# Two of the last batch's transposes moved from TensorE to the DMA engines

## The chip, the cores and the metric

The kernel runs on one core of one Trainium2 chip. The metric is the device time of one execution in microseconds, the median of several runs. A profile of one execution goes with it. In it PE is TensorE's matmul row and PEld its row of weight loads, DVE is VectorE, ACT is ScalarE, POOL is GpSimd, and SP is SyncE, which here only issues DMAs.

## The reference

Two layers stand one behind the other. The first is a causal linear attention with decay over 4 batches, 8 heads, 768 tokens and 64 channels a head, in blocks. The second takes its output x, with the heads laid side by side (4 x 768 x 512), and mixes tokens with weights that are made from x:

```python
# lightning attention, per block of 64 tokens
intra = ((qb @ kb.T) * Dmask) @ vb
inter = (qb * lam_pow) @ kv_state
out[:, :, sl] = intra + inter
kv_state = lam_block * kv_state + (kb * rev_pow).T @ vb

# token mixer
wq, wk = x @ w_q, x @ w_k                   # 512 -> 64
W_tok = scale * einsum('bsd,btd->bst', wq, wk)
mixed = einsum('bst,btd->bsd', W_tok, x)
out = maximum(mixed, 0) @ w_out             # 512 -> 512
```

## The kernel before

**Tiles.** The 32 heads are worked as 16 pairs, numbered n = 4 b + kk: batch b has the pairs 4b to 4b+3. A pair has 128 channels (two heads of 64) and 768 tokens, in six chunks of 128. For a pair the kernel loads q, k and v (DMAs issued by GpSimd that also convert to bf16), turns q and k with TensorE so that channels lie on partitions, makes scores, masks them, makes states, and sums the inner and the outer part in PSUM. `attended` (word `ex`) copies the result into xnat[b], with tokens on partitions. The mixer's projections need x with channels on partitions as well, so `flip` (word `F`, line 427) transposes the six chunks of a pair on TensorE into PSUM, and `flipped` (word `ef`, line 235 through the helper `copy`) copies them into xT[b].

**The mixer of a batch.** `mix_q` (word `Q`, line 449) multiplies xT, four matmuls for the four pairs of a batch in the order kk = 0 to 3, for each half of the tokens; `mix_k` (`K`, line 475) turns a part back to tokens on partitions; `mix_y` (`Y`, line 500) multiplies that with xnat; `mix_m` (`m`, line 524) makes the mixed values, and `mixed_m` (`em`, lines 535 and 537) applies the relu into rmT[b]; `mix_o` (`O`, line 553) multiplies with w_out, and `mixed_o` (`eo`) copies a tile of 128 tokens and stores it by a DMA on SyncE's queue (line 564).

**Two orders of tokens.** q is loaded in a way that puts neighbouring tokens, even and odd, side by side in a row of SBUF. So within a chunk the tokens of one kind stand in the kernel in another order ("the order of the q loads") than in the output. `flip` multiplies with the matrix `order`, not with the identity `ident`, and so puts the tokens of xT back into the order of the output while it transposes. `mix_k` then reads every second column to fit xT to xnat again.

**What sets the order.** It is written by hand: the string ORDER is a list of words, `name.arguments@PSUM-bank:engine`, and each word emits its instructions in that place. Each engine runs its own instructions strictly in order; semaphores hold an instruction until its inputs are there. There are no planned costs or due times. The change concerns the last five lines of ORDER: the pairs 12 to 15 are those of the last batch, b = 3, whose attention ends beside the last mixing steps of batch 2. Its `Q.3.1` and `Q.3.0` are the first words that read xT[3].

The words around the change, with the lines of the profile:

- `ex.12`, `ex.13` and `ex.14` run on ScalarE (`:a`), `ex.15` on VectorE (`:v`); all are line 235, tile xnat.
- `F.12` to `F.15` are line 427; `ef.12` and `ef.14` run on ScalarE, `ef.13` and `ef.15` on VectorE.
- `m.2.0` to `m.2.3` and `em.2.0` to `em.2.3` are the last products and relus of batch 2, `O.1.2` an output tile of batch 1 kept for this place.
- `Q.3.1`, `Q.3.0`, `K.3`, `Y.3` and the words `m.3` and `O.3` are batch 3's mixer, with the output tiles of batch 2 in the gaps.

Of the kernel before, what the change touches and what calls it, by code (L numbers as in the profile page):

```python
# [9 lines left out]
BF16 = mybir.dt.bfloat16  # L10
F32 = mybir.dt.float32
ALU = mybir.AluOpType
ACT = mybir.ActivationFunctionType

B, H, S, D = 4, 8, 768, 64
CH = 128
NCH = S // CH
HD = H * D
DHY = 64
NP = H // 2  # L20
HALF = 3 * CH
# [9 lines left out]
v.13 sv.10:p q.14 k.14 v.14 sv.11:p q.15 k.15 v.15 sv.12:p sv.13:p sv.14:p hold.14 Aq.0@0 dq.2  # L31
eq.0@0 dq.1 Z.5@7 Ak.0@0 dq.3 ek.0@0:v Z.3@7 S0.0@0 sv.0:v S1.0@2 Mc.1.0@2 M0.0@0 Z.3@7 Pw.0@4
Aq.1@5 G.0@4:a Mm.1.0:v Z.1@7 I.0@0 eq.1@5 V.0@0 Ak.1@5 ex.0@0:a ek.1@5:v Z.2@7 F.0@4 sv.1:v
S0.1@0 M0.1@0 Z.1@7 Aq.2@5 Pw.1@2 eq.2@5 G.1@2:a Z.1@7 Ak.2@3 ef.0@4:v S1.1@0 ek.2@3:v M1.1@0
Z.1@7 S0.2@2 S1.2@4 I.1@6 Mc.0.2@2 V.1@6 sv.2:v Mc.1.2@4 Z.1@3 Aq.3@2 ex.1@6:a Mm.1.2:v Pw.2@3
eq.3@2 Ak.3@4 G.2@3:a Mm.0.2:v F.1@5 ek.3@4:a I.2@2 ef.1@5:v V.2@2 sv.3:v S0.3@4 cw.0:a S1.3@6
Qp.0.0@0 Mc.1.3@6 M0.3@4 Pw.3@1 Aq.4@6 G.3@1:a Mm.1.3:v I.3@4 ex.2@2:v V.3@4 Qp.1.0@1 ex.3@4:a
Ak.4@7 eq.4@6 F.2@2 ek.4@7:a F.3@6 ef.2@2:v Qp.0.1@0 eg.3.0@6:a Qp.1.1@1 Qp.0.2@0 eg.3.1@6:v
Qp.0.3@0 Qp.1.2@1 eQ.0.0@0:a Qp.1.3@1 S0.4@6 eQ.0.1@1:a S1.4@2 M0.4@6 Mc.1.4@2 Kh.0.1@1 Kh.0.0@0
Aq.5@4 Ak.5@5 ek2.0.1@1:v ek2.0.0@0:a Mm.1.4:v Y.0@0 ek.5@5:a eq.5@4 YA.0@0:a YB.0@0:v S1.5@4  # L40
M1.5@4 YC.0@0:a m.0.1@1@2 Pw.4@3 eh.0.1.1@2:a m.0.0@0@6 eh.0.1.0@1:v G.4@3:a Aq.6@2 eh.0.0.1@6:a
I.4@4 eq.6@2 eh.0.0.0@0:a S0.5@6 m.0.3@1@3 M0.5@6 V.4@4 eh.0.3.1@3:a Ak.6@2 ex.4@4:a sv.6:v
m.0.2@3@0 eh.0.2.0@3:a F.4@4 ek.6@2:a eh.0.2.1@0:v P.6@3 P.5@5 Gp.6@3 eh.0.3.0@1:a S0.6@6 O.0.4@2
Gp.5@5 Mc.0.6@6 ef.4@4:v S1.6@6 eo.0.4@2:a I.6@0 Mm.0.6:v I.5@4 V.5@4 M1.6@6 Aq.7@2 ex.5@4:a
Ak.7@3 eq.7@2 O.0.5@6 ek.7@3:v V.6@0 eo.0.5@6:v S1.7@2 S0.7@4 M1.7@2 F.5@6 O.0.0@7 ex.6@0:v
O.0.3@2 eo.0.0@7:a M0.7@4 O.0.1@7 ef.5@6:v F.6@3 sv.8:v eo.0.1@7:a P.7@6 Ak.8@4 ef.6@3:a Gp.7@6
Aq.8@7 P.8@5 ek.8@4:a eq.8@7 I.7@0 V.7@0 Gp.8@5 Aq.9@4 ex.7@0:a eo.0.3@2:v Ak.9@5 S0.8@6 ek.9@5:v
# [9 lines left out]
Q.2.0@0 Mc.1.12@6 Q.2.1@1 Mm.0.13:v eQ.2.0@0:a P.13@4 Mm.1.12:v Ak.15@5 eQ.2.1@1:a Gp.13@4 Aq.15@0  # L57
ek.15@5:a Ak.14@1 eq.15@0 Aq.14@4 ek.14@1:a sv.15:v K.2@6 Pw.14@0 eK.2@6:a S0.15@2 eq.14@4 P.12@1
Mc.0.15@2 Y.2@5 Gp.12@1 G.14@0:a P.15@4 YB.2@5:v YA.2@5:a I.13@2 S1.15@0 Gp.15@4 S0.14@6 YC.2@5:a
V.13@2 Mc.0.14@6 M1.15@0 O.1.0@4 ex.13@2:a Mm.0.14:v I.15@0 S1.14@6 Mm.0.15:v eo.1.0@4:a I.12@2  # L60
V.12@2 M1.14@6 V.15@0 ex.12@2:a I.14@4 ex.15@0:v m.2.3@6 V.14@4 F.12@2 em.2.3@6:v ex.14@4:a F.15@3
F.13@0 ef.12@2:a ef.15@3:v F.14@1 m.2.1@6 ef.13@0:v ef.14@1:a m.2.0@4 m.2.2@2 em.2.0@4:v O.1.2@0
em.2.2@2:a Q.3.1@1 em.2.1@6:a Q.3.0@2 eo.1.2@0:a eQ.3.1@1:v O.2.3@3 eQ.3.0@2:a K.3@2 eo.2.3@3:a
O.2.5@0 eK.3@2:v Y.3@1 eo.2.5@0:a O.2.1@0 YA.3@1:v YB.3@1:a YC.3@1:v m.3.0@2 eo.2.1@0:v m.3.1@6
m.3.2@4 em.3.0@2:a O.2.2@1 em.3.2@4:v em.3.1@6:a m.3.3@2 eo.2.2@1:v O.2.0@0 em.3.3@2:a O.2.4@1
eo.2.0@0:v O.3.0@2 eo.2.4@1:a O.3.1@3 eo.3.0@2:a O.3.4@2 eo.3.1@3:a O.3.3@3 eo.3.4@2:v O.3.5@1
eo.3.3@3:a O.3.2@0 eo.3.5@1:a eo.3.2@0:a
"""
# [3 lines left out]
def kernel(  # L72
# [11 lines left out]
    nc = tc.nc  # L84
    mm = nc.tensor.matmul

    consts = ctx.enter_context(tc.tile_pool(name="consts", bufs=1))
    stage = ctx.enter_context(tc.tile_pool(name="stage", bufs=N))
    tsb = ctx.enter_context(tc.tile_pool(name="tsb", bufs=4))
    small = ctx.enter_context(tc.tile_pool(name="small", bufs=2))  # L90
    big = ctx.enter_context(tc.tile_pool(name="big", bufs=2))
# [4 lines left out]
    PS = ps.tile([128, 8, HD], F32, name="ps")  # L96
    PSH = PS.bitcast(BF16)
# [42 lines left out]
    def load_wo(_):  # L140
# [28 lines left out]
        out=ET[:, 0:CH], data0=step, data1=step, initial=0.0, op0=ALU.add, op1=ALU.bypass  # L169
    )  # L170
    for at, n in ((CH, CH), (2 * CH, 2 * CH), (4 * CH, 2 * CH)):
        nc.vector.tensor_tensor(
            out=ET[:, at : at + n], in0=ET[:, 0:n],
# [3 lines left out]
    ident = consts.tile([128, 128], BF16, name="ident")  # L177
    nc.vector.tensor_tensor(
        out=ident.rearrange("e (p r) -> e p r", r=2), in0=natural,
# [4 lines left out]
        out=mask1, in0=ET[:, 0:CH], in1=row.to_broadcast([128, CH]), op=ALU.is_ge  # L184
# [4 lines left out]
    for r in range(2):  # L189
        nc.vector.tensor_tensor(  # L190
            out=token[R[r], :], in0=token[R[r], :],
# [5 lines left out]
        out=order.rearrange("e (p r) -> e p r", r=2), in0=natural,  # L197
# [5 lines left out]
        out=E6, in0=ET[:, ::CH], in1=row.to_broadcast([128, NCH]), op=ALU.add  # L203
# [3 lines left out]
    lamv = lam_all.rearrange("p (k l) -> p k l", l=2)  # L207
    for hl in range(2):
        nc.scalar.activation(out=lncol[R[hl], :], in_=lamv[R[hl], :, hl], func=ACT.Ln)
    pw48 = consts.tile([128, H, NCH], F32, name="pw48")  # L210
    mask2 = mask1.unsqueeze(1).unsqueeze(1).to_broadcast([128, 2, 3, CH])
    Dq = [consts.tile([128, S], BF16, name=f"dq{kk}") for kk in range(NP)]
# [18 lines left out]
    qT, kT, pr, gs = {}, {}, {}, {}  # L231
    xnat, xT = {}, {}

    def copy(eng, to, of):
        return (nc.scalar.copy if eng == "a" else nc.vector.tensor_copy)(out=to, in_=of)  # L235
# [94 lines left out]
    def masked(a):  # L330
        def one(n, o):
            pr[n, a] = tsb.tile([128, 2, HALF], BF16, tag=f"pr{a}", name="pr")
            nc.vector.tensor_tensor(  # L333
                out=pr[n, a].rearrange("j l (c i) -> j l c i", c=3),
                in0=PS[:, o : o + 2, 0:HALF].rearrange("j l (c i) -> j l c i", c=3),
                in1=mask2,
                op=ALU.mult,
            )

        return one  # L340
# [10 lines left out]
        )  # L351


    def states(whole):
        def one(n, o):
            to = PS[:, o, 0 : (NCH - 1) * D].rearrange("e (c f) -> e c f", c=NCH - 1)
            for c in range(NCH - 1):
                end = 2 if c < 2 and not whole else NCH - 1
                for hl in range(2):
                    mm(  # L360
                        to[R[hl], c:end, :],
                        fk[n][:, hl, c, :],
                        vn[n][:, hl, c, :].unsqueeze(1).to_broadcast([128, end - c, D]),
                        start=(c == 0),
                        stop=(c == NCH - 2),
                        skip_group_check=True,
                    )

        return one

    def summed(n, o, eng):
        gs[n] = tsb.tile([128, NCH - 1, D], BF16, tag="gs", name="gs")
        of = PS[:, o, 0 : (NCH - 1) * D].rearrange("e (c f) -> e c f", c=NCH - 1)
        copy(eng, gs[n], of)

    def added(n, o):
        gs[n] = tsb.tile([128, NCH - 1, D], BF16, tag="gs", name="gs")
# [46 lines left out]
    def flip(n, o):  # L424
        b, kk = divmod(n, NP)
        for c in range(NCH):
# [3 lines left out]
                order,  # L430
            )

    def flipped(n, o, eng):
        b, kk = divmod(n, NP)
        copy(eng, xT[b][:, kk, :], PSH[:, o, 0:S])
# [8 lines left out]
    qk, wkn, YA, YB, rmT = {}, {}, {}, {}, {}  # L444
# [24 lines left out]
            qk[b] = small.tile([128, S], BF16, tag="qk", name="qk")  # L469
        copy(eng, qk[b][:, n * HALF : (n + 1) * HALF], PS[:, o, 0:HALF])  # L470

    def mix_k(b, o, chunks=range(NCH)):
        for c in chunks:
            for r in range(2):
                mm(
                    PS[R[r], o, c * DHY : (c + 1) * DHY],
                    qk[b][:, c * CH + r : (c + 1) * CH : 2],
                    ident[:, R[1 - c // 3]],
                    start=(c == chunks[0]),
                    stop=(c == chunks[-1]),  # L480
                    skip_group_check=True,
                )

    def mix_k_half(b, half, o):
        mix_k(b, o, range(3 * half, 3 * half + 3))
# [27 lines left out]
    def crossed_y(f):  # L513
        def one(b, o, eng):
            if b not in YB:
                YB[b] = small.tile([128, 256], BF16, tag="YB", name="YB")
            copy(eng, YB[b][R[1 - f], :], PS[R[f], o, 0:256])

        return one
# [13 lines left out]
    def relu(eng, to, of):  # L533
        if eng == "a":
            nc.scalar.activation(out=to, in_=of, func=ACT.Relu, scale=1.0 / 8.0)  # L535
        else:
            nc.vector.tensor_scalar(
                out=to, in0=of, scalar1=1.0 / 8.0, scalar2=0.0, op0=ALU.mult, op1=ALU.max
            )

    def mixed_m(b, dd, o, eng):
        if b not in rmT:
            rmT[b] = big.tile([128, 4, 2, HALF], BF16, tag="rmT", name="rmT")
        relu(eng, rmT[b][:, dd], PS[:, o : o + 2, 0:HALF])

    def mixed_m_half(b, dd, n, o, eng):
        if b not in rmT:
            rmT[b] = big.tile([128, 4, 2, HALF], BF16, tag="rmT", name="rmT")
        relu(eng, rmT[b][:, dd, n], PS[:, o, 0:HALF])
# [40 lines left out]
    def zeros(count, o):  # L590
# [9 lines left out]
        q=load_q, k=load_k, v=load_v, wq=load_wq, wk=load_wk, cw=copy_wq, wo=load_wo, hold=hold, dq=make_dq, dv=make_dv,  # L600
        sv=scale_v, Aq=turn_q, Ak=turn_k, eq=turned_q, ek=turned_k, A4q=turn_q4, A4k=turn_k4,
        e4q=turned_q4, e4k=turned_k4, S0=scores(0), S1=scores(1),
        M0=masked(0), M1=masked(1), Mc=drawn, Mm=masked_late, P=states(False), Pw=states(True), G=summed, Gp=added, I=inter, V=values, ex=attended, F=flip,
        ef=flipped, eg=flipped_half, Q=mix_q, eQ=mixed_q, K=mix_k, eK=mixed_k, Kh=mix_k_half, ek2=mixed_k_half, Y=mix_y, YA=mixed_y, YB=crossed_y(0), YC=crossed_y(1), Qp=mix_q_part, m=mix_m,
        em=mixed_m, eh=mixed_m_half, O=mix_o, eo=mixed_o, Oh=mix_o_half, oh=mixed_o_half, Z=zeros,
    )
    for word in ORDER.split():
        piece, _, eng = word.partition(":")
# [34 lines left out]
```

## Time and profile before

| | |
|---|---|
| time, median of 3 runs | 101.39 us (101.31 to 101.42) |
| span of the profiled execution | 99.9 us |
| first load issued by GpSimd / last flip ends, by the chain of waits | 1.24 us / 80.03 us |
| flips on TensorE in all | 96 matmuls, 7.3 us busy |
| copies of flips | VectorE 10 of 552 ns, ScalarE 5 of 805 ns, and two halves |
| stores of the output on SyncE's queue | 24, 256 KB each, 2.0 us from issue to landing |

A busy share is an average over the whole span. What the change can be worth is read from the chain of waits, which goes back from the last instruction to what released each, and from the timeline of the stretch from 75 to 85 us, in which the attention of the last four pairs ends and the mixer of the last batch begins.

The line of DMA shares of the page gives the state of the DMA engines in 40 equal slices, in tenths:

```profile
DMA  0999999999999999999999999999910202526782
```

The loads keep all 16 engines at nine tenths until slice 29, that is until about 72 us. After it there are stores alone.

### The profile page before, as it was taken

To read this page: it belongs to the slowest core of one execution; us is meant where nothing else is said; L and a number is where in the kernel's file an instruction comes from. 1 tells how busy PE (TensorE), PEld (TensorE's weight loads), DVE (VectorE), ACT (ScalarE), POOL (GpSimd) and SP (SyncE) were. 2 spreads that over 40 slices of the span, in tenths; PEclk is the share of its full clock that TensorE was granted. 3 is DMA by queue.
4 is the path that set the end of the run, shared out by engine and by line. 5 is a ranking of instruction groups with operands and counts; after the bars stand their busy time and mean duration, and the time that the engine had idled before them with its cause. 6 is when DMAs were issued, how large, how long until landed. Compare 5 with 4: busy or idle time off the path is not lost.

```text
span 99.9 us, 3414 instructions
## 1 busy us (share of the span) xinstructions
PE 90.6 (91%) x1458; PEld 59.4 (59%) x1466; DVE 74.3 (74%) x145; ACT 65.2 (65%) x107; POOL 62.2 (62%) x65
## 2 busy tenths in 40 slices
PE   5999999799998779999999999999999999999930
PEld 3465777678555445757858675866976854434400
DVE  6739596988686996799999899787999964482200
ACT  5585414676877924326798898888978895484440
POOL 5999995889989998999999999940000000000000
PEclk9999999999999966999999999999999999999999
DMA  0999999999999999999999999999910202526782
GB/s 1 98 141 161 164 159 166 161 163 166 164 162 200 173 167 159 165 171 156 164 167 163 163 170 161 162 317 403 361 35 7 105 7 105 210 105 243 282 315 105
DMA packets 67438, 16.60 MB, mean 166 GB/s; under 512 B 63840, under 2 KB 64352, under 8 KB 67424
## 3 DMA queue, kind: packets, MB, share of 16 engines
q0 software_dynamic: 63792, 10.10, 136.8%
q1 hardware_dynamic: 3632, 6.30, 16.8%
q8 instruction: 11, 0.18, 0.7%
q14 instruction: 3, 0.02, 0.1%
HBM read 20.19 MB, written 6.29 MB: 265 GB/s over the span
## 4 chain that ended last, share of the span: by engine, by line
PE 42%; DVE 20%; POOL 20%; DMA 8%; issue 4%; ACT 1%; POOLq 0%; DVEq 0%; ACTq 0%
PE ps L553 18%; DMA fv<-in_v_dram 8%; POOL fk L118 6%; POOL fv L122 6%; POOL fq L114 5%; DVE pr L333 4%; PE ps L360 3%; PE ps L319 3%; DVE fv L240 3%; PE ps L404 3%; PE ps L449 3%; PE ps L524 3%; PE ps L427 2%; DVE pr L349 2%; DVE qT L308 2%
## 5 line engine op out<-in xcount | busy, mean ns | idle before, releaser
L553 PE MATMUL ps<-wo,rmT 128*128 128x512 bf16 x88 | 23.2, 388 | 0.7 <-issue 0.4
L122 POOL DMA_DIRECT2D fv<-in_v_dram x16 | 16.6, 1039 | 2.3 <-DMA fv<-in_v_dram 1.4
L333 DVE TENSOR_TENSOR pr<-ps,mask 128x768 bf16<-128x768 f32 x17 | 16.1, 951 | 1.8 <-PE ps L319 1.8
L235 ACT COPY osb<-ps 128x512 f32<-128x512 f32 x18 | 10.6, 588 | 10.3 <-PE ps L553 10.2
L118 POOL DMA_DIRECT2D fk<-in_k_dram x16 | 16.8, 1049 | 0.3 <-DMA fv<-in_v_dram 0.3
L345 ACT CAST pr<-ps 128x768 bf16<-128x768 f32 x15 | 11.7, 803 | 4.8 <-PE ps L319 4.7
L114 POOL DMA_DIRECT2D fq<-in_q_dram x16 | 14.1, 884 | 0.8 <-POOLq L627 0.8
L553 PEld LDWEIGHTS <-rmT 128*128 128x128 bf16 x96 | 8.6, 99 | 9.7 <-issue 1.3
L240 POOL TENSOR_TENSOR fv<-fv,DvI 128x768 bf16<-128x768 bf16 x9 | 14.0, 1572 | 0.0
L235 ACT CAST xnat<-ps 128x768 bf16<-128x768 f32 x12 | 9.6, 800 | 4.3 <-PE ps L404 4.2
L593 PE MATMUL ps<-blank 128*128 128x128 f32 (+3 forms) x26 | 10.5, 514 | 1.1 <-DVE blank L159 1.1
L308 DVE TENSOR_TENSOR qT<-ps,dq 128x768 bf16<-128x768 bf16 x16 | 8.8, 551 | 1.7 <-PE ps L252 1.5
L349 DVE TENSOR_TENSOR pr<-pr,mask 128x768 bf16<-128x768 bf16 x15 | 9.9, 668 | 0.2
L535 ACT ACTIVATE rmT<-ps 128x768 bf16<-128x768 f32 (+1 forms) x14 | 9.0, 677 | 1.1 <-PE ps L524 0.9
L319 PE MATMUL ps<-qT,kT 64*128 64x128 bf16 x192 | 9.4, 223 | 0.4
L360 PE MATMUL ps<-fv,fk 128*64 128x128 bf16 (+4 forms) x160 | 8.1, 236 | 1.8 <-DVE fv L240 1.3
L252 PE MATMUL ps<-ident,fq 128*64 128x128 bf16 x192 | 8.2, 221 | 0.6 <-DMA fq<-in_q_dram 0.5
L360 PEld LDWEIGHTS <-fk 128*64 128x64 bf16 x160 | 6.4, 114 | 3.9 <-DVE fv L240 1.4
L240 DVE TENSOR_TENSOR fv<-fv,DvI 128x768 bf16<-128x768 bf16 x7 | 7.9, 1134 | 0.7 <-DMA fv<-in_v_dram 0.6
L319 PEld LDWEIGHTS <-kT 64*128 64x128 bf16 x192 | 5.8, 96 | 4.1 <-issue 1.9
L261 PE MATMUL ps<-ident,fk 128*64 128x128 bf16 x192 | 8.2, 221 | 0.0
L404 PE MATMUL ps<-fv,pr 128*128 128x64 bf16 x192 | 8.1, 194 | 0.0
(68 smaller groups left out, 143.8 us busy)
## 6 DMA issues: line engine op xcount, KB each, us to landing
out_dram<-osb SPq DMA_DIRECT2D x24, 256.0 KB, 2.0
fq<-in_q_dram POOLq DMA_DIRECT2D x16, 192.0 KB, 8.0
fk<-in_k_dram POOLq DMA_DIRECT2D x16, 192.0 KB, 8.4
fv<-in_v_dram POOLq DMA_DIRECT2D x16, 192.0 KB, 8.5
wo<-in_moe_w_out_dram POOLq DMA_DIRECT2D x1, 512.0 KB, 9.9
wqk<-in_moe_w_q_dram POOLq DMA_DIRECT2D x1, 64.0 KB, 7.9
wqk<-in_moe_w_k_dram POOLq DMA_DIRECT2D x1, 64.0 KB, 7.6
lam_all<-in_lam_dram SPq DMA_DIRECT2D x1, 4.0 KB, 2.5
```

The costliest lines, as they stand in the source:

```text
L114: nc.gpsimd.dma_start(out=fq[n], in_=rows_q(n))
L118: nc.gpsimd.dma_start(out=fk[n], in_=rows(n, k))
L122: nc.gpsimd.dma_start(out=fv[n], in_=rows(n, v))
L235: return (nc.scalar.copy if eng == "a" else nc.vector.tensor_copy)(out=to, in_=of)
L240: (nc.gpsimd if eng == "p" else nc.vector).tensor_tensor(out=vn[n], in0=fv[n], in1=DvI[:, 2 * kk : 2 * kk + 2, :].unsqueeze(3).to_broadcas ...
L319: mm(PS[:, o + hl, cc * CH : (cc + 1) * CH], kT[n][R[hl], c], qT[n][R[hl], c], start=True, stop=True, skip_group_check=True,)
L333: nc.vector.tensor_tensor(out=pr[n, a].rearrange("j l (c i) -> j l c i", c=3), in0=PS[:, o : o + 2, 0:HALF].rearrange("j l (c i) -> j l c ...
L345: nc.scalar.copy(out=pr[n, a], in_=PS[:, o : o + 2, 0:HALF])
L349: (nc.gpsimd if eng == "p" else nc.vector).tensor_tensor(out=of, in0=of, in1=mask2, op=ALU.mult)
L360: mm(to[R[hl], c:end, :], fk[n][:, hl, c, :], vn[n][:, hl, c, :].unsqueeze(1).to_broadcast([128, end - c, D]), start=(c == 0), stop=(c == ...
L404: mm(PS[:, o + hl, c * D : (c + 1) * D], pr[n, c // 3][:, hl, (c % 3) * CH : (c % 3 + 1) * CH], vn[n][:, hl, c, :], start=False, stop=(c = ...
L553: mm(PS[:, o, :], rmT[b][:, kt].rearrange("f n i -> f (n i)")[:, t * CH : (t + 1) * CH], wo[:, kt, :], start=(kt == 0), stop=(kt == 3),)
```

## The change

Pairs 12 and 13 are no longer transposed by TensorE. `flip_dma` (word `DF`) issues six DMA transposes a pair on SyncE's queue, each from a 128 x 128 piece of xnat[3] in SBUF straight into xT[3] in SBUF, behind the copies `ex.13` and `ex.12`. The words `F.12`, `F.13`, `ef.12` and `ef.13` are gone. The purpose is to use the DMA engines, which have little to do once the loads have ended, for work that now takes TensorE, a PSUM bank, and a copy on VectorE or ScalarE.

[...] So the whole last batch stays in the order of the q loads: pairs 14 and 15 are flipped with `ident` (`flip_plain`, word `Fi`), `mix_k` reads two contiguous runs of columns in place of every second one (`mix_k_plain`, word `Kc`), and the relu puts the tokens back in order as it writes rmT (`mixed_m_plain`, word `en`), with a step of two elements.

```diff
-V.13@2 Mc.0.14@6 M1.15@0 O.1.0@4 ex.13@2:a Mm.0.14:v I.15@0 S1.14@6 Mm.0.15:v eo.1.0@4:a I.12@2
-V.12@2 M1.14@6 V.15@0 ex.12@2:a I.14@4 ex.15@0:v m.2.3@6 V.14@4 F.12@2 em.2.3@6:v ex.14@4:a F.15@3
-F.13@0 ef.12@2:a ef.15@3:v F.14@1 m.2.1@6 ef.13@0:v ef.14@1:a m.2.0@4 m.2.2@2 em.2.0@4:v O.1.2@0
+V.13@2 Mc.0.14@6 M1.15@0 O.1.0@4 ex.13@2:a DF.13 Mm.0.14:v I.15@0 S1.14@6 Mm.0.15:v eo.1.0@4:a I.12@2
+V.12@2 M1.14@6 V.15@0 ex.12@2:a DF.12 I.14@4 ex.15@0:v m.2.3@6 V.14@4 em.2.3@6:v ex.14@4:a Fi.15@3
+ef.15@3:v Fi.14@1 m.2.1@6 ef.14@1:a m.2.0@4 m.2.2@2 em.2.0@4:v O.1.2@0
...
+    def flip_dma(n):
+        b, kk = divmod(n, NP)
+        for c in range(NCH):
+            nc.sync.dma_start_transpose(
+                out=xT[b][:, kk, c * CH : (c + 1) * CH],
+                in_=xnat[b][:, c, kk * CH : (kk + 1) * CH],
+            )
...
+                if plain:
+                    at = slice(c * CH + r * D, c * CH + (r + 1) * D)
...
+        relu(
+            eng,
+            rmT[b][:, dd].rearrange("f n (c p r) -> f n c r p", c=3, r=2),
+            PS[:, o : o + 2, 0:HALF].rearrange("f n (c r p) -> f n c r p", c=3, r=2),
+        )
```

In the rest of the last batch `K.3` becomes `Kc.3` and the four `em.3` become `en.3`. Two memsets of a small tile `keep` are added at the start; together with two further helpers (`scanned` and the form "single" of `states`) they belong to words that ORDER does not use.

More of the change, by code (lines that the diff above doesn't have):

```diff
@@ L59 @@
 Mc.0.15@2 Y.2@5 Gp.12@1 G.14@0:a P.15@4 YB.2@5:v YA.2@5:a I.13@2 S1.15@0 Gp.15@4 S0.14@6 YC.2@5:a
-V.13@2 Mc.0.14@6 M1.15@0 O.1.0@4 ex.13@2:a Mm.0.14:v I.15@0 S1.14@6 Mm.0.15:v eo.1.0@4:a I.12@2
-V.12@2 M1.14@6 V.15@0 ex.12@2:a I.14@4 ex.15@0:v m.2.3@6 V.14@4 F.12@2 em.2.3@6:v ex.14@4:a F.15@3
-F.13@0 ef.12@2:a ef.15@3:v F.14@1 m.2.1@6 ef.13@0:v ef.14@1:a m.2.0@4 m.2.2@2 em.2.0@4:v O.1.2@0
-em.2.2@2:a Q.3.1@1 em.2.1@6:a Q.3.0@2 eo.1.2@0:a eQ.3.1@1:v O.2.3@3 eQ.3.0@2:a K.3@2 eo.2.3@3:a
+V.13@2 Mc.0.14@6 M1.15@0 O.1.0@4 ex.13@2:a DF.13 Mm.0.14:v I.15@0 S1.14@6 Mm.0.15:v eo.1.0@4:a I.12@2
+V.12@2 M1.14@6 V.15@0 ex.12@2:a DF.12 I.14@4 ex.15@0:v m.2.3@6 V.14@4 em.2.3@6:v ex.14@4:a Fi.15@3
+ef.15@3:v Fi.14@1 m.2.1@6 ef.14@1:a m.2.0@4 m.2.2@2 em.2.0@4:v O.1.2@0
+em.2.2@2:a Q.3.1@1 em.2.1@6:a Q.3.0@2 eo.1.2@0:a eQ.3.1@1:v O.2.3@3 eQ.3.0@2:a Kc.3@2 eo.2.3@3:a
 O.2.5@0 eK.3@2:v Y.3@1 eo.2.5@0:a O.2.1@0 YA.3@1:v YB.3@1:a YC.3@1:v m.3.0@2 eo.2.1@0:v m.3.1@6
-m.3.2@4 em.3.0@2:a O.2.2@1 em.3.2@4:v em.3.1@6:a m.3.3@2 eo.2.2@1:v O.2.0@0 em.3.3@2:a O.2.4@1
+m.3.2@4 en.3.0@2:a O.2.2@1 en.3.2@4:v en.3.1@6:a m.3.3@2 eo.2.2@1:v O.2.0@0 en.3.3@2:a O.2.4@1
 eo.2.0@0:v O.3.0@2 eo.2.4@1:a O.3.1@3 eo.3.0@2:a O.3.4@2 eo.3.1@3:a O.3.3@3 eo.3.4@2:v O.3.5@1
@@ L209 @@
         nc.scalar.activation(out=lncol[R[hl], :], in_=lamv[R[hl], :, hl], func=ACT.Ln)
+    keep = consts.tile([128, NCH - 1], F32, name="keep")
+    nc.vector.memset(keep, 1.0)
+    nc.vector.memset(keep[:, 0:1], 0.0)
     pw48 = consts.tile([128, H, NCH], F32, name="pw48")
@@ L351, in masked_late, with states @@
         )
-    def states(whole):
+    def states(form):
         def one(n, o):
@@ L357, in one @@
             for c in range(NCH - 1):
-                end = 2 if c < 2 and not whole else NCH - 1
+                end = NCH - 1
+                if form == "halves" and c < 2:
+                    end = 2
+                if form == "single":
+                    end = c + 1
                 for hl in range(2):
@@ L374, in summed, with scanned @@
         copy(eng, gs[n], of)
+    def scanned(n, o):
+        gs[n] = tsb.tile([128, NCH - 1, D], BF16, tag="gs", name="gs")
+        nc.vector.tensor_tensor_scan(
+            out=gs[n].rearrange("e c f -> e f c"),
+            data0=keep.unsqueeze(1).to_broadcast([128, D, NCH - 1]),
+            data1=PS[:, o, 0 : (NCH - 1) * D].rearrange("e (c f) -> e f c", c=NCH - 1),
+            initial=0.0,
+            op0=ALU.mult,
+            op1=ALU.add,
+        )
     def added(n, o):
@@ L431, in flip, with flip_plain @@
             )
+    def flip_plain(n, o):
+        b, kk = divmod(n, NP)
+        for c in range(NCH):
+            nc.tensor.transpose(
+                PSH[:, o, c * CH : (c + 1) * CH],
+                xnat[b][:, c, kk * CH : (kk + 1) * CH],
+                ident,
+            )
+    def flip_dma(n):
+        b, kk = divmod(n, NP)
+        for c in range(NCH):
+            nc.sync.dma_start_transpose(
+                out=xT[b][:, kk, c * CH : (c + 1) * CH],
+                in_=xnat[b][:, c, kk * CH : (kk + 1) * CH],
+            )
     def flipped(n, o, eng):
@@ L470, in mixed_q, with mix_k @@
         copy(eng, qk[b][:, n * HALF : (n + 1) * HALF], PS[:, o, 0:HALF])
-    def mix_k(b, o, chunks=range(NCH)):
+    def mix_k(b, o, chunks=range(NCH), plain=False):
         for c in chunks:
             for r in range(2):
+                at = slice(c * CH + r, (c + 1) * CH, 2)
+                if plain:
+                    at = slice(c * CH + r * D, c * CH + (r + 1) * D)
                 mm(
                     PS[R[r], o, c * DHY : (c + 1) * DHY],
-                    qk[b][:, c * CH + r : (c + 1) * CH : 2],
+                    qk[b][:, at],
                     ident[:, R[1 - c // 3]],
@@ L482, in mix_k, with mix_k_plain @@
                 )
+    def mix_k_plain(b, o):
+        mix_k(b, o, plain=True)
     def mix_k_half(b, half, o):
@@ L544, in mixed_m, with mixed_m_plain @@
         relu(eng, rmT[b][:, dd], PS[:, o : o + 2, 0:HALF])
+    def mixed_m_plain(b, dd, o, eng):
+        if b not in rmT:
+            rmT[b] = big.tile([128, 4, 2, HALF], BF16, tag="rmT", name="rmT")
+        relu(
+            eng,
+            rmT[b][:, dd].rearrange("f n (c p r) -> f n c r p", c=3, r=2),
+            PS[:, o : o + 2, 0:HALF].rearrange("f n (c r p) -> f n c r p", c=3, r=2),
+        )
     def mixed_m_half(b, dd, n, o, eng):
@@ L602 @@
         e4q=turned_q4, e4k=turned_k4, S0=scores(0), S1=scores(1),
-        M0=masked(0), M1=masked(1), Mc=drawn, Mm=masked_late, P=states(False), Pw=states(True), G=summed, Gp=added, I=inter, V=values, ex=attended, F=flip,
+        M0=masked(0), M1=masked(1), Mc=drawn, Mm=masked_late, P=states("halves"), Pw=states("whole"), Ps=states("single"), Gs=scanned, G=summed, Gp=added, I=inter, V=values, ex=attended, F=flip,
         ef=flipped, eg=flipped_half, Q=mix_q, eQ=mixed_q, K=mix_k, eK=mixed_k, Kh=mix_k_half, ek2=mixed_k_half, Y=mix_y, YA=mixed_y, YB=crossed_y(0), YC=crossed_y(1), Qp=mix_q_part, m=mix_m,
-        em=mixed_m, eh=mixed_m_half, O=mix_o, eo=mixed_o, Oh=mix_o_half, oh=mixed_o_half, Z=zeros,
+        em=mixed_m, eh=mixed_m_half, Fi=flip_plain, DF=flip_dma, Kc=mix_k_plain, en=mixed_m_plain, O=mix_o, eo=mixed_o, Oh=mix_o_half, oh=mixed_o_half, Z=zeros,
     )
```

## The prediction

> **What bounds the kernel now.** I read the engine shares first, then the chain of waits, then the timeline of the part that the change touches.
>
> ```profile
> PE 90.6 (91%) x1458; PEld 59.4 (59%) x1466; DVE 74.3 (74%) x145; ACT 65.2 (65%) x107; POOL 62.2 (62%) x65
> ...
> PE 42%; DVE 20%; POOL 20%; DMA 8%; issue 4%; ACT 1%; POOLq 0%; DVEq 0%; ACTq 0%
> ```
>
> The share of 91% is an average over stages, so it does not tell what ends the last stage. The chain in order of time does. Its columns are start, length, and what.
>
> ```profile
> 78.64 1.40 PE ps L427 x24
> 80.03 0.59 PE ps L524 x6
> 80.63 0.33 PE ps L553
> 80.96 0.05 issue
> 81.02 0.59 PE ps L553 x2
> 81.61 1.30 PE ps L449 x8
> ...
> 88.84 7.04 PE ps L553 x32
> 95.88 0.03 ACTq L235
> ```
>
> From about 64 us on nearly every piece of the chain is TensorE. The 24 flips (line 427, four pairs of six chunks) stand in it with 1.40 us, so twelve of them look like 0.70 us on the path. That reading has to be checked: a chain charges an engine's own queue even where an engine was about to wait anyway. I therefore read what the flips wait for. First ScalarE, then the weight loads of the flips, each with start, length, engine and line:
>
> ```profile
> 75.76 0.81 ACT L235 CAST xnat<-ps 128x768 bf16<-128x768 f32 x1
> ...
> 77.43 0.80 ACT L235 CAST xnat<-ps 128x768 bf16<-128x768 f32 x1 [0.38 <-PE ps L404]
> ...
> 78.67 0.80 ACT L235 CAST xnat<-ps 128x768 bf16<-128x768 f32 x1 [0.44 <-PE ps L404]
> ```
> ```profile
> 78.44 1.02 PEld L427 LDWEIGHTS <-xnat 128*128 128x128 bf16 x18
> ...
> 79.52 0.34 PEld L427 LDWEIGHTS <-xnat 128*128 128x128 bf16 x6
> ```
>
> The three copies on ScalarE are those of pairs 13, 12 and 14. The copy of pair 14 ends at 78.67 + 0.80 = 79.47. The first 18 weight loads (pairs 12, 15, 13) end at 79.46; the last six, pair 14's, begin at 79.52, that is 0.05 us after the copy. So pair 14's flip waits for that copy already now, and the flips of pairs 12 and 13 fill the time before it.
>
> **What the Trainium skill says.** "DMA: Bandwidth & Descriptors", section "Two DMAs through the same engine are not ordered", says that only the completion count of a DMA tells that its data is there, so the reader of a DMA's output waits for a landing, not for an issue. The trace agrees in kind: stores take 2.0 us from issue to landing, though their issue takes 0.33 us. The page "VectorE: DVE Perf Modes", section "The three transpose paths", prices a 128x128 bf16 transpose by DMA at 1309 ns; no DMA transpose is in this trace. "DMA: Bandwidth & Descriptors", section "Why a DMA increments its semaphore by 16 and not by 1", compares sequencer times of the generation before trn3: 512 cycles for a plain DMA, 631 for a small DMA transpose from HBM. The trace has only the former, and here the source is SBUF. "TensorE: Matmul & The Clock Gate", section "What's actually happening", says that TensorE falls to half clock after an idle window of some 3.4 us; the windows of this trace show 1.00 from 60 us on and no such gap.
>
> **The change part by part.**
>
> TensorE loses 12 flips: 12 x 0.056 us (18 loads begin over 1.02 us) = 0.70 us of its work. On the path they are worth almost nothing. Pair 15's flip may begin when VectorE's copy ends, about 78.74 us, and takes 6 x 0.056 = 0.34 us to 79.1. Pair 14's flip still waits for 79.47. It begins at 79.52 as before. After it the order is the same: six products of line 524, one output tile (line 553), then the projections of line 449, which begin at 81.44 in the timeline. I take 0 to 0.05 us gained.
>
> ScalarE loses a copy of 0.81 us (pair 12) and VectorE one of 0.55 us (pair 13). ScalarE's copy of pair 14's flip is still released by that flip, which does not move; the relus behind it are queued from there. VectorE's relu could start near 80.5 instead of 80.58, and the last relu before the output tiles is on ScalarE. Value 0.
>
> The relus of the last batch now write in steps of two elements. No row shows such a write. From below it costs 0 (the read side, 768 elements from PSUM in 0.81 us, is the same); from above it doubles the three ScalarE relus at 87.23 to 89.69 us. Their first reader is the output tiles of the last batch; eight matmuls of other tiles (8 x 0.22 us from 88.84) stand ahead, to 90.6, so up to 0.9 us is hidden. I take 0. Reading qk without the step of two in line 475 and the other identity matrix in the flips cost nothing: same sizes. The two added memsets (columns of five and one) lie on VectorE before its product with ScalarE's logarithm, in the wait for that: 0.
>
> What is added is 12 DMA transposes on SyncE's queue, and a wait: the first projection (line 449) begins with pair 12's rows of xT, the ones that come last. TensorE runs in order, so all else is queued behind it: the second projection, the output tiles of batch 2, the whole of batch 3. The time is then set by the landing of the twelfth transpose. SyncE's row now:
>
> ```profile
> L564 SPq DMA_DIRECT2D out_dram<-osb x24: 332/333/1590, 63.2 to 96.6; - x24
> ...
> DMA to landing us min/median/max: 2.0/2.0/5.9
> ```
>
> An issue takes 0.33 us. Between two issues in a row (68.64 with a length of 0.60, then 69.33) lie 0.09 us more, so one DMA costs SyncE 0.42 us. Pair 13's transposes may start at 75.76 + 0.81 + 0.05 = 76.62. Queue: six transposes, one store, six transposes; pair 12's data (78.23) is there by then.
> - From below, a transpose priced as a store: twelve starts of 0.42 after the first give 81.66; +2.0 landing, +0.05 = 83.71, against 81.44: a wait of 2.27 us, so 103.7.
> - With the ratio 631/512 of the skill: issue 0.41, with 0.09 a pitch of 0.50: 11 x 0.50 + 0.42 = 5.92, last start 82.54, landing and wake 84.59: a wait of 3.15 us, so **104.5**. An estimate, but the one that I take: a transpose has more descriptors to make than a row copy, and this is the smallest price above a store's.
> - From above, 1.309 us each with no overlap: 12 x 1.309 = 15.7, with the rest of a 2.0 us landing (0.7): 93.0; a wait of 11.6 us, so 113.0, and more with a cold clock.
>
> Behind the transposes on SyncE wait the stores of the output tiles from 82 us on. Each DMA on this queue also waits for the eighth before it to have landed; at 0.50 us apart that one is 4.0 us old, so a landing of 2.0 us doesn't hold it up. The 12 output buffers leave room, and the queue is empty again before the last stores at 96.6: 0.
>
> **The rivals.**
> 1. In time: all twelve land by 81.4. That needs 11p + 0.42 + 2.0 at most 4.8 us, so p of 0.22 us, half of a store's pitch, or a landing much below 2.0 us. SBUF to SBUF could land sooner, which speaks for it; the row of issues speaks against. Time: 101.3 to 101.4. This is the side that is not slower; there is little to win, since pair 14's copy keeps its date. That would be "the same" rather than "faster", unless the emptier VectorE and ScalarE shift more than I see (101.1).
> 2. Dearer, partly overlapped: p of 0.75 us, twice a store's work. 11 x 0.75 + 0.42 = 8.67, last start 85.29, landed 87.3: a wait of 5.9 us. After 3.4 us of it TensorE would be at half clock and run some 3.4 us so; half of that, 1.7 us, is lost. 101.4 + 5.9 + 1.7 = 109.0.
> 3. One after another at 1.309 us: 113.0, with the clock 114.7. For it: the skill's price. Against it: a single transpose's price can be mostly latency, which overlaps, as the 2.0 us of a store do behind issues every 0.42.
>
> **How the numbers follow.** Issue-bound as computed, 103.5 to 106: 0.50. Rival 2, 106 to 110: 0.18. Rival 3: 0.15. Rival 1: 0.17, of which 0.12 the same and 0.05 faster. Predicted 104.5, the likeliest. The range goes from 101.3, most of rival 1, to 110.0, the end of rival 2; left out are rival 3 and the faster tail, 0.2 in all. It reaches over the store's price and the ratio's price, and of the 1.309 us it takes in as much as two in flight at once. Slower 0.83, same 0.12, faster 0.05.
>
> **What would show it.** Right: twelve issues on SyncE from 76.6 us with a pitch near 0.5; the projections (mix_q) of the last batch begin after an idle stretch of TensorE that ends on a DMA of xT, near 84.5; the pair 14 flip still begins at 79.5; all after it shifted by one amount. Wrong: the projections begin at 81.4 with no wait (rival 1), the landings come over 1 us apart (rival 3), or the granted clock after the wait is below 1.00 (rival 2). A relu that takes 1.6 us would show that I was wrong on the strided write. I would be wrong altogether if pair 14's flip began before 79.4.

## The result, and the profile after

The changed kernel takes 115.54 us (median of 4, 115.06 to 116.64) against 101.36 us before (median of 4): a ratio of 1.141, 95% interval 1.133 to 1.150. It is slower by 14.2 us. The forecast was slower by 3.1 us, with a range that ended at 110. Most of the kernels here, the unchanged one too, have some executions that take 2% to 5% longer; the ratios leave these out, and two of the profiles below (one instruction for a pair, TensorE kept busy) are of such executions, with a low clock before 48 us and the full clock in the stretches compared here.

The granted clock of TensorE in 40 slices, and the chain of waits by engine and by line, from the page of the changed kernel:

```profile
PEclk9999999999999999999999679999997555999999
...
PE 35%; POOL 17%; SPq 12%; DVE 11%; DMA 8%; issue 7%; ACT 6%; DVEq 0%; POOLq 0%; ACTq 0%
PE ps L606 16%; SPq L466 11%; DMA fq<-in_q_dram 6%; POOL fk L118 5%; POOL fv L122 5%; POOL fq L114 4%; PE ps L487 4%; DVE pr L336 3%; PE ps L322 3%; DVE fv L243 2%; PE ps L423 2%; ACT pr L348 2%; DMA xT<-xnat 2%; PE ps L446 2%; PE ps L368 2%
```

A new name stands in the chain: SPq, SyncE's queue, with 12% of the span, nearly all of it line 466, the DMA transposes. "DMA xT<-xnat", the landing of the last one, is only 2%. By the chain the time goes into issuing, not into moving; the first two experiments test that. The same line's own row and its landings:

```profile
L466 SPq DMA_TRANSPOSE xT<-xnat x12: 1094/1227/1232, 77.8 to 92.4; - x12
...
DMA to landing us min/median/max: 2.2/2.3/2.4
```

Each of the twelve occupies SyncE for some 1.23 us (the median), where the median store took 0.33 us. The data is there 2.3 us after the beginning of an issue, so 1.1 us after its end. The timeline shows who waited:

```profile
80.77 0.51 PE L456 MATMUL ps<-ident,xnat 128*128 128x128 bf16 x6 [0.22 <-ACT xnat L238]
...
94.77 2.74 PE L487 MATMUL ps<-xT,wqk 128*128 128x384 bf16 x8 [11.94 <-DMA xT<-xnat]
```

Pair 14's flip waits for ScalarE's copy, as before. The projections then begin after 11.94 us of idle TensorE, and their eight matmuls, 1.46 us before, take 2.74. Why they take longer is in the windows (length; PE, PEld, DVE, ACT, POOL busy; granted clock; DMA share; GB/s):

```profile
88.00:92.00 4.00, 0.00 (x0) 0.00 (x0) 0.00 (x0) 0.00 (x0) 0.00 (x0) 0.50 0.12 25
92.00:96.00 4.00, 1.23 (x4) 0.59 (x5) 0.00 (x0) 0.00 (x0) 0.00 (x0) 0.50 0.28 86
96.00:100.00 4.00, 4.00 (x30) 1.78 (x30) 1.11 (x2) 1.20 (x3) 0.00 (x0) 0.78 0.00 0
```

In the wait the clock falls to half, and it is back only in the window from 96 us. Narrower windows put the half clock from 87.49 to 97.73 us. It begins 4.65 us after TensorE's last work, and 2.96 us of the work behind the wait fall into it. At half clock that costs half of 2.96, an estimate of 1.48 us.

Three distances account for the difference of the two profiled executions, whose spans are 99.9 and 114.4 us. In each profile I take the start of pair 14's copy into xnat, the start of the last batch's projections, and the end of the last copy of an output tile.

| | before | after | difference |
|---|---|---|---|
| start to pair 14's copy | 78.67 | 79.91 | +1.24 |
| pair 14's copy to the projections | 2.77 | 14.86 | +12.09 |
| projections to the last output copy | 15.09 | 16.53 | +1.44 |

The line for the start of the projections before, then the last output copy before and, last, after:

```profile
81.44 1.46 PE L449 MATMUL ps<-xT,wqk 128*128 128x384 bf16 x8
...
95.95 0.58 ACT osb L235
...
110.72 0.58 ACT osb L238
```

The last 0.3 us of the difference, with the other sign, lie behind the last copy. The first row of the table lies ahead of anything that waits for a transpose, and is taken not to be the change's: in the changed kernel's profile the clock was also low near 64 to 67 us, among the loads; in that of before near 36 to 39 us. The profiled execution was also the longest of the changed kernel's four; the spans of the other three are 113.1 to 113.7 us, that is 13.2 to 13.8 us above 99.9. The two other rows sum to 13.5 us.

### The profile page after: what moved, and what is told of

It is laid out like the page before. It is cut to its first block, busy times and chain, and to the rows that moved or that the text cites. A ratio compares the mean times of both kernels' runs of the same rounds, so it can differ in the third digit from the quotient of the medians.

```text
span 114.4 us, 3412 instructions
## 1 busy us (share of the span) xinstructions
PE 92.5 (81%) x1454; PEld 59.7 (52%) x1454; DVE 74.5 (65%) x146; ACT 65.0 (57%) x106; POOL 62.0 (54%) x65
## 3 DMA queue, kind: packets, MB, share of 16 engines
q1 hardware_dynamic: 5552, 6.69, 16.3%
## 4 chain that ended last, share of the span: by engine, by line
PE 35%; POOL 17%; SPq 12%; DVE 11%; DMA 8%; issue 7%; ACT 6%; DVEq 0%; POOLq 0%; ACTq 0%
PE ps L606 16%; SPq L466 11%; DMA fq<-in_q_dram 6%; POOL fk L118 5%; POOL fv L122 5%; POOL fq L114 4%; PE ps L487 4%; DVE pr L336 3%; PE ps L322 3%; DVE fv L243 2%; PE ps L423 2%; ACT pr L348 2%; DMA xT<-xnat 2%; PE ps L446 2%; PE ps L368 2%
## 5 line engine op out<-in xcount | busy, mean ns | idle before, releaser
L606 PE MATMUL ps<-wo,rmT 128*128 128x512 bf16 x96 | 24.1, 392 | 0.1
L487 PE MATMUL ps<-xT,wqk 128*128 128x384 bf16 x24 | 5.7, 392 | 12.0 <-DMA xT<-xnat 11.9
L243 POOL TENSOR_TENSOR fv<-fv,DvI 128x768 bf16<-128x768 bf16 x9 | 13.8, 1542 | 0.0
L352 DVE TENSOR_TENSOR pr<-pr,mask 128x768 bf16<-128x768 bf16 x15 | 11.1, 753 | 0.4 <-ACT pr L348 0.2
L238 ACT CAST qk<-ps 128x384 bf16<-128x384 f32 x7 | 3.2, 486 | 14.2 <-PE ps L487 13.7
L487 PEld LDWEIGHTS <-wqk 128*128 128x128 bf16 x24 | 2.6, 112 | 14.6 <-DMA xT<-xnat 12.4
L579 ACT ACTIVATE rmT<-ps 128x768 bf16<-128x768 f32 (+1 forms) x14 | 9.5, 724 | 1.0 <-PE ps L568 0.9
L238 DVE CAST qk<-ps 128x384 bf16<-128x384 f32 x1 | 0.6, 557 | 13.6 <-PE ps L487 13.6
L322 PE MATMUL ps<-qT,kT 64*128 64x128 bf16 x192 | 8.8, 218 | 0.2
L423 PE MATMUL ps<-fv,pr 128*128 128x64 bf16 x192 | 8.7, 200 | 0.0
```

The lines of the kernel that those rows point to most:

```text
L243: (nc.gpsimd if eng == "p" else nc.vector).tensor_tensor(out=vn[n], in0=fv[n], in1=DvI[:, 2 * kk : 2 * kk + 2, :].unsqueeze(3).to_broadcas ...
L322: mm(PS[:, o + hl, cc * CH : (cc + 1) * CH], kT[n][R[hl], c], qT[n][R[hl], c], start=True, stop=True, skip_group_check=True,)
L352: (nc.gpsimd if eng == "p" else nc.vector).tensor_tensor(out=of, in0=of, in1=mask2, op=ALU.mult)
L487: mm(PS[:, o, 0:HALF], wqk[:, kt, n * DHY : n * DHY + 2 * DHY], xT[b][:, kt, n * HALF : (n + 1) * HALF], start=(kt == 0), stop=(kt == 3),)
L606: mm(PS[:, o, :], rmT[b][:, kt].rearrange("f n i -> f (n i)")[:, t * CH : (t + 1) * CH], wo[:, kt, :], start=(kt == 0), stop=(kt == 3),)
```

## Experiments

The theory after the result: an instruction of this kind costs SyncE 1.23 us whatever it moves, twelve stand in a row ahead of the projections, and behind the wait TensorE runs at half clock for a while. The rivals were a price by bytes, a disturbance of other work, and a price in the other parts of the change. Each time has its own kernel of before beside it; that one's median was 101.5 to 101.8 us. Medians are over all runs. In the diffs of ORDER only the words around an edit are printed, as parts of longer lines.

### One instruction for a pair

xnat of the last batch is laid out pair by pair (`by_pair`), so one transpose can take a pair's six chunks. The other places that write or read xnat follow the new layout; they are not printed.

```diff
...
-        for c in range(NCH):
-            nc.sync.dma_start_transpose(
-                out=xT[b][:, kk, c * CH : (c + 1) * CH],
-                in_=xnat[b][:, c, kk * CH : (kk + 1) * CH],
-            )
+        nc.sync.dma_start_transpose(
+            out=xT[b][:, kk, :].rearrange("f (c i) -> f c i", c=NCH),
+            in_=by_pair(xnat[b])[:, kk].rearrange("i c e -> i (c e)"),
+        )
...
```

> One DMA transpose for a whole pair in place of six for its chunks: xnat of the last batch is laid out pair by pair, so that a pair's six chunks are 768 columns in a row. 2 instructions on SyncE for the same bytes. Theory A (SyncE's time goes with the amount that it transposes): each instruction occupies SyncE for 6 x 1.23 = 7.4 us, pair 12 lands as late as before, 114 to 116 us. Theory B (the 1.23 us are mostly a fixed price of an instruction): each takes 1.3 to 2 us, both have landed before 82 us, and the time is 101.2 to 102.0 us. Between them, at about 3 to 4 us each, 104 to 107 us.

Measured: 101.18 us, ratio 0.996 (0.994 to 0.998). The row of the transposes and their landings:

```profile
L470 SPq DMA_TRANSPOSE xT<-xnat x2: 1257/1280/1302, 80.5 to 82.5; - x2
...
DMA to landing us min/median/max: 2.8/2.8/2.8
```

Six times the data in one instruction costs 1.28 us instead of 1.23, and lands 0.5 us later. That is theory B of this expectation. The whole loss of the change is gone with the same bytes moved by the same engines: pair 14's copy to the projections is 2.76 us again, and from there to the last output copy it is 15.09 us. There is no time to spare, for the second transpose lands just as the projections are due: their weight load still waits 0.29 us for it.

### Pieces of half the size

```diff
         for c in range(NCH):
-            nc.sync.dma_start_transpose(
-                out=xT[b][:, kk, c * CH : (c + 1) * CH],
-                in_=xnat[b][:, c, kk * CH : (kk + 1) * CH],
-            )
+            for r in range(2):
+                nc.sync.dma_start_transpose(
+                    out=xT[b][:, kk, c * CH + r * D : c * CH + (r + 1) * D],
+                    in_=xnat[b][R[r], c, kk * CH : (kk + 1) * CH],
+                )
```

> The changed kernel with each piece cut in two (64 tokens by 128 channels): 24 instructions of half the size. Theory A (the price is fixed for an instruction): each takes SyncE 1.2 us, the last is issued some 15 us later than in the changed kernel, 130 to 132 us. Rival (the price goes with size below one piece): 0.6 to 0.7 us each, 115 to 117 us.

Measured: 131.25 us in one run, against a median of 101.64 us before.

```profile
L467 SPq DMA_TRANSPOSE xT<-xnat x24: 1089/1226/1227, 76.4 to 106.1; - x24
```

A piece of half the size still takes 1.226 us. From 64 x 128 over 128 x 128 to 128 x 768 elements the price is 1.226, 1.227 and 1.280 us: nearly fixed for the instruction, in this range. It doesn't follow the number of packets that the DMA engines move either. The profiles count 3632 packets on the queue of the stores before, and 5936, 5552 and 5232 with the 24, 12 and 2 transposes, so that one transpose makes 96, 160 and 800.

### Pair 13 alone by DMA

```diff
-ex.12@2:a DF.12 I.14@4 ex.15@0:v m.2.3@6 V.14@4 em.2.3@6:v ex.14@4:a Fi.15@3
-ef.15@3:v Fi.14@1
+ex.12@2:a I.14@4 ex.15@0:v m.2.3@6 V.14@4 Fi.12@2 em.2.3@6:v ex.14@4:a Fi.15@3
+ef.12@2:a ef.15@3:v Fi.14@1
```

> Only pair 13 by DMA transposes, pair 12 flipped on TensorE with the identity. Theory A (the wait is for the last piece in SyncE's queue, each piece 1.27 us): start 76.6, the sixth issued at 83.0, landed at 85.3 against 81.5 for the second matmul of the projection, so a wait of 3.8 us and 105.0 to 105.6 us, 106.5 if TensorE's clock drops. Rival (the cost is the transfers' disturbance of other work, or a price of the first use): more than half of the 14 us stays, 108 us or more.

Measured: 107.66 us (106.94 to 109.56), ratio 1.058 (1.052 to 1.064): 5 to 6 us slower, above what was expected of theory A.

```profile
82.36 0.33 PE L487 MATMUL ps<-xT,wqk 128*128 128x384 bf16 x1
...
86.30 2.42 PE L487 MATMUL ps<-xT,wqk 128*128 128x384 bf16 x7 [3.60 <-DMA xT<-xnat]
```

The first projection matmul reads pair 12 and runs on time; the second reads pair 13 and would follow 0.16 us later, at 82.52. It waits until 86.30, so 3.78 us, the 3.8 expected. What was under-estimated is the clock: the projections to the last output copy take 20.25 us, and 20.25 - 15.09 - 3.78 = 1.38 us is nearly the whole clock loss of the twelve, after an idle stretch of only 3.6 us. The granted clock agrees: it is 0.50 from 85.72 us, 3.03 us into the idle stretch, to 89.14, and 2.84 us of work fall into that, 1.42 us lost by half of it. In this profile pair 14's copy also begins 0.93 us later than before, ahead of the wait; that part is not explained here. With the 24 half pieces TensorE waits 27.3 us, the clock is 0.50 from 85.09 to 112.40, 3.66 us of work fall into that, and the stretch behind the wait takes 16.86 us, 1.77 above 15.09. So in these three kernels the loss goes with how much work falls into the half clock, and not with how long the wait before it was.

### TensorE kept busy in the wait

```diff
-em.2.2@2:a Q.3.1@1
+em.2.2@2:a Z.44@5 Q.3.1@1
```

> The changed kernel with 44 x 128 columns of dummy matmuls (11 matmuls of 512 columns in f32, about 0.85 us each, on a free bank) ahead of the last batch's projections, inside the wait of 12 us. Theory A (of the 14 us, some 1.4 us are work after the wait at half clock): 113.5 to 114.5 us, and the clock is 1.00 from the wait to the end. Rival (the wait alone makes the loss, the clock none): 115.5 us as the changed kernel. If the dummies last longer than the wait, over 116 us.

Measured: 113.84 us (113.46 to 117.14), ratio 1.119 (1.113 to 1.126), against 1.141 of the change. The same window as above, in this kernel:

```profile
96.00:100.00 4.00, 3.14 (x27) 1.67 (x28) 1.10 (x2) 1.06 (x2) 0.00 (x0) 1.00 0.20 70
```

The clock is 1.00, as in all windows from 84 to 104 us. Pair 14's copy to the projections is 14.86 us, to the hundredth that of the change, and from there to the last output copy it is 15.10 us in place of 16.53. Before the change it was 15.09. The ratios differ by some 2.2 us, give or take 1, which agrees. So 1.43 us of the loss are the low clock, and the wait is untouched by it.

### The change without its DMA transposes

```diff
-ex.13@2:a DF.13 Mm.0.14:v ... ex.12@2:a DF.12 I.14@4
+ex.13@2:a Mm.0.14:v ... ex.12@2:a I.14@4
...
-V.14@4 em.2.3@6:v ex.14@4:a Fi.15@3
-ef.15@3:v Fi.14@1 m.2.1@6 ef.14@1:a
+V.14@4 Fi.12@2 em.2.3@6:v ex.14@4:a Fi.15@3
+Fi.13@0 ef.12@2:a ef.15@3:v Fi.14@1 m.2.1@6 ef.13@0:v ef.14@1:a
```

> All else of the change without the DMA transposes: the last batch stays in the order of the q loads, all four pairs flipped on TensorE with the identity, projections' reads contiguous, relus writing in steps of two. Theory A (these parts cost nothing that shows): 101.3 to 101.5 us. Rival (the relus' strided writes, three on ScalarE and one on VectorE, slow the last batch): 101.7 to 102.3 us.

Measured: 101.34 us, ratio 0.994 (0.991 to 0.997). The relus before, and with strided writes:

```profile
87.23 2.46 ACT L535 ACTIVATE rmT<-ps 128x768 bf16<-128x768 f32 x3 [0.48 <-PE ps L524]
...
86.54 2.79 ACT L579 ACTIVATE rmT<-ps 128x768 bf16<-128x768 f32 x3 [0.48 <-PE ps L568]
```

Three take 2.79 us where they took 2.46, 0.11 us more each. Projections to the last output copy remain 15.08 us, so that is hidden. The other parts of the change cost nothing that shows. Whether a DMA transpose could write with a step of two, and so do without the plain order, was not tried. The small gain is taken up below.

### No flips of pairs 12 and 13 at all

```diff
+    def no_flip(b):
+        nc.gpsimd.memset(xT[b][:, 0:2, :], 0.0)
...
-ex.13@2:a Mm.0.14:v
+ex.13@2:a NF.3 Mm.0.14:v
...
-V.14@4 F.12@2 em.2.3@6:v ex.14@4:a F.15@3
-F.13@0 ef.12@2:a ef.15@3:v F.14@1 m.2.1@6 ef.13@0:v ef.14@1:a
+V.14@4 em.2.3@6:v ex.14@4:a F.15@3
+ef.15@3:v F.14@1 m.2.1@6 ef.14@1:a
```

> The kernel before without the flips of pairs 12 and 13 and their two copies, and nothing in their place: these rows of xT hold zeros that GpSimd writes behind its last work, so the last batch's projections read zeros there (this part of the computation is left out). Theory A (pair 14's flip waits for ScalarE's copy of pair 14, the two flips fill that wait): 101.3 to 101.5 us, and the projections begin 2.77 us after that copy begins, as before. Rival (the chain's reading: 12 flips of 0.056 us are on the path): 100.6 to 100.8 us, projections 2.1 us after the copy's begin.

Measured: ratio 1.002 (0.998 to 1.006), median 102.08 us. The kernel leaves out the part of the projections that needs these flips. TensorE's row around the flips, and the copy that one of them waits for:

```profile
78.09 0.80 ACT L235 CAST xnat<-ps 128x768 bf16<-128x768 f32 x1 [0.45 <-PE ps L404]
78.21 0.51 PE L427 MATMUL ps<-order,xnat 128*128 128x128 bf16 x6 [0.16 <-DVE xnat L235]
...
78.94 0.51 PE L427 MATMUL ps<-order,xnat 128*128 128x128 bf16 x6 [0.23 <-ACT xnat L235]
```

With both flips gone pair 14's flip still begins 0.05 us after its copy ends at 78.89, and TensorE is idle 0.16 us and 0.23 us where it flipped before. The projections come 2.76 us after the copy's begin, in place of 2.77. The 0.70 us that the chain seems to offer are worth nothing, even for free.

### Two pieces of pair 13 by DMA

```diff
-        for c in range(NCH):
+        for c in range(2):
             nc.sync.dma_start_transpose(
```

The other four chunks of pair 13 and all of pair 12 are flipped on TensorE.

> Two of pair 13's six pieces by DMA transposes, the other four and pair 12 flipped on TensorE. Both are issued by 79.2 us and land about 80.2 us, before the projections. Theory A (what cost time is the number of instructions on SyncE, and below some three of them are free): 101.2 to 101.5 us, no wait on a DMA. Rival (a DMA transpose as such disturbs TensorE or the DMA queue's other work): over 102 us.

Measured: ratio 0.996 (0.994 to 0.999), median 101.41 us. The two are issued at 75.9 and 77.1 us and land in 2.3 us; no engine waits for them. A transpose that lands in time does no harm.

### Two pairs of batch 2, beside the loads

Words of the pairs 8 and 9 only; batch 2 takes the plain order too, and the last batch is flipped on TensorE.

```diff
-eK.1@2:a ex.8@6:a Y.1@2
+eK.1@2:a ex.8@6:a DF.8 Y.1@2
...
-ex.9@0:a P.10@7
+ex.9@0:a DF.9 hold.14 st.0.4 st.0.5 st.0.0 st.0.1 st.0.3 st.0.2 P.10@7
```

> A try at a gain: the pairs 8 and 9 of batch 2 are transposed by one DMA transpose each, some 10 us before their projections, with xnat of batch 2 laid out pair by pair and batch 2 in the order of the q loads as well; all of the last batch is flipped on TensorE in that order. The stores of the first six output tiles are put behind these two on SyncE's queue, where a wait for k of pair 14 held them until 62 us anyway. Theory A (a flip is worth its 0.34 us where TensorE is not about to wait; pair 8's flips lie in the stretch that is all TensorE from 66 us on, pair 9's in one that VectorE sets): 0.3 to 0.7 us faster than before, 100.6 to 101.0 us. Rival (beside the loads a transpose lands too late or slows the loads): 101.3 us or more, and a wait of the projections on the DMA if it lands late.

Measured: ratio 0.995 (0.991 to 0.998), but a median of 102.72 us over 22 runs from 100.54 to 105.93, against 101.64 before. The two point in opposite directions, so no gain is shown. A window of the kernel with two pieces of pair 13, the same window here, and the landings here:

```profile
58.00:62.00 4.00, 3.81 (x78) 2.47 (x75) 3.79 (x6) 3.63 (x6) 4.00 (x4) 1.00 2.23 163
...
58.00:62.00 4.00, 3.51 (x60) 2.03 (x55) 3.70 (x8) 2.99 (x5) 4.00 (x4) 1.00 2.22 121
...
DMA to landing us min/median/max: 8.6/8.9/9.1
```

Beside the loads a transpose of 128 x 768 lands after 8.6 to 9.1 us, not 2.8. And the loads suffer: from 58 to 62 us the DMA engines move 121 GB/s, in the kernel with two pieces 163 GB/s in that stretch, and SyncE's small DMA that waits for k of pair 14 goes out at 66.9 us in place of 62.1 us. In these profiles the copy of pair 14 begins at 79.02 us here and at 78.00 us there. So what the flips left free on TensorE does not show as an earlier end; the loads came later. That the transposes, and not the changed dates of the stores, delay the loads fits the time of the dip; it was not tried alone. In the profile of before the loads' own packets end by 67 us; what fills the DMA line from there to 72 us are stores.

### Is the plain order a little faster?

Three kernels with the plain order had measured 0.994 to 0.996. The two edits left to suspect were taken one by one: the memsets alone on the kernel before, and the plain order without them.

```diff
+    keep = consts.tile([128, NCH - 1], F32, name="keep")
+    nc.vector.memset(keep, 1.0)
+    nc.vector.memset(keep[:, 0:1], 0.0)
```

> The kernel before with nothing but the change's two small memsets on VectorE at the start. Asked: three kernels with the plain order and these memsets measured 0.994 to 0.996 of before, though their profiles do the stretch from pair 14's copy to the end in the same 17.85 us as before. Theory C (the memsets or the start's dates shift when TensorE's clock falls in the load stretch): 0.994 to 0.997 of before. Theory D (the plain order is faster): 0.999 to 1.001.

> The plain order with all flips on TensorE, without the two memsets. Theory C (memsets): 0.999 to 1.001 of before. Theory D (plain order): 0.993 to 0.997. If both this and the memsets alone give 0.994 to 0.998, or neither does, the difference is one of when the clock falls, which these runs don't tie to an edit.

Measured: 0.998 (0.995 to 1.001) for the memsets, 1.001 (0.998 to 1.004) for the plain order without them. Neither alone gives the 0.6% of both. The medians of all runs hardly show a difference either: the plain order with the memsets has 101.34 us against 101.54, without them 101.65 against 101.84, both 0.998, and the memsets alone 101.89 against 101.84. So a gain of 0.6% is not shown, and there is no cause to look for. No kernel here can be called faster than before by an edit that explains it. The one with one transpose for a pair, 101.18 us, is 12% below the change and within half a per cent of before, and the kernel with the flips on TensorE is as good.

## Why the prediction was wrong

- **The direction and the path were right.** TensorE waits for the twelfth landing ahead of the projections; pair 14's flip keeps its date (80.77, 0.06 us behind its copy's end at 80.71); all behind the projections is shifted, and takes 1.44 us longer by the clock. That the twelve flips are worth almost nothing on the path was read from one gap of 0.05 us in the weight loads, and leaving them out showed it. (Their sum, 12 x 0.056, is 0.67 us and not 0.70, which is half of the chain's 1.40; nothing hangs on it.)
- **The term that failed is the pitch of SyncE.** "A pitch of 0.50" came from a store's 0.33 us times 631/512, from the Trainium skill's page "DMA: Bandwidth & Descriptors", section "Why a DMA increments its semaphore by 16 and not by 1". Measured is 1.23 us of issue, 1.27 us from start to start: 3.7 times a store's issue and not 1.23 times, so the page's ratio, given for small transposes from HBM on "previous generations", does not hold for these from SBUF. The reason given, "the smallest price above a store's", was a choice of the cheap end where no row of the trace showed the operation; and that a transpose has more descriptors to make doesn't set the price, for 96 packets and 800 cost about the same. With 1.27 the sum of the prediction gives 11 x 1.27 + 0.63 for the store between, 14.6 us, and with 2.37 us for the last landing and 0.05 to wake it ends at 94.8 us from a start at 77.8 us: the 94.77 of the profile. The forecast wait was 3.15 us, the measured one 12.09. Of the 8.94 us between them 11 x 0.77, or 8.5 us, are the pitch; the later landing (2.37 us for 2.0) and the store between make up the rest.
- **Rival 3 had the size, not the mechanism.** It took the 1309 ns of the page "VectorE: DVE Perf Modes", section "The three transpose paths", as transfers one after another, and its 113.0 and 114.7 us are near the result: its landings over 1 us apart and rival 2's low clock are the signs that came. But the transfers do overlap, 2.3 us each at starts 1.27 us apart. The chip pays about that price, but per instruction and on SyncE: six chunks in one instruction cost about the same, half a chunk too. So the rival's figure came near by another price, which is luck. I doubted the rival because a landing's latency overlaps; the latency does overlap, the issue does not. Its 15% were left out of the range, and the result with them.
- **The clock was put at nothing in the forecast, and filed under the rivals.** 1.7 us was estimated for a wait of over 3.4 us, from the page "TensorE: Matmul & The Clock Gate", section "What's actually happening"; 1.43 us was measured, and an idle stretch of 3.6 us already costs 1.38. The traces agree with the page in kind: the clock fell 3.03 us into one idle stretch and 4.65 us into the other. The predicted wait of 3.15 us was so near to that bound that it should have been weighed there.
- **The strided relus** were put between 0 and a doubling: 0.11 us each measured, and hidden, as taken.
- **The store that stands between the two groups** took 0.52 us rather than 0.33. With its gap that is 0.63 us in place of 0.42, two tenths of a microsecond, and changes little.

## What to carry to other kernels

Before work is moved off the engine that the chain names, ask what the next instruction on it waits for: here twelve flips stood in the chain with 0.70 us and leaving them out gained nothing. Price a DMA by its issue as well as by its transfer, and where the trace has no row for it, measure one instruction first, or let the range hold the dearest price. Where the issue is a fixed price, lay the data out so that one instruction takes all of it: two transposes of 768 columns cost SyncE about what two of 128 do. All transposes here were issued by SyncE; whether the price is the same on another engine's queue was not tried.

## What the runs showed of the hardware

- A DMA transpose from SBUF to SBUF occupied SyncE for 1.226 us at 64 x 128, 1.227 at 128 x 128 and 1.28 us at 128 x 768 elements in bf16 (medians); a store of 256 KB occupied it for 0.33 us.
- With the loads over it landed 2.3 us after the start of its issue (2.8 us for 128 x 768); beside the loads one of 128 x 768 took 8.6 to 9.1 us.
- After an idle stretch of 3.6 us, or of 11.9 us, TensorE's work behind it took about 1.4 us more. After one of 27.3 us it was 1.8 us. The granted clock was 0.50 for 3.42, 10.24 and 27.31 us in the three, about one, three and eight times the same length. It began 3.0 to 4.7 us into the idle stretch, and half of the work that fell into it (2.84, 2.96 and 3.66 us) is the loss, to within 0.06 us. Dummy matmuls in the wait took the loss away.
